# Banks for the output projection's transposes, scores of the last groups, a third begun step and halved sums in an attention + MLP kernel

## Chip, cores and metric

One core of one Trainium2 chip runs the whole program. The metric is device time in microseconds (us) of one execution. The engines are TensorE (PE, with its weight loads as PEld), VectorE (DVE), ScalarE (ACT), GpSimd (POOL) and SyncE (SP), which issues the DMAs. PE writes its results to PSUM, which has eight banks of 128 rows x 512 fp32 values; DVE and ACT read them there.

## What is computed

A pre-norm transformer layer in fp32: 2048 tokens, width 512, 32 heads of 16, and an MLP of width 1792 with SiLU.

```python
def _A_ref(x, wqkv, wo):                       # attention
    qkv = (x @ wqkv).reshape(B, S, 3, H, Dh).transpose(2, 0, 3, 1, 4)
    q, k, v = qkv[0], qkv[1], qkv[2]
    p = softmax(einsum("bhqd,bhkd->bhqk", q, k) * Dh ** -0.5)
    o = einsum("bhqk,bhkd->bhqd", p, v)
    return o.transpose(0, 2, 1, 3).reshape(B, S, D) @ wo
def _B_ref(x, w1, w2):                         # MLP
    return silu(x @ w1) @ w2
h  = x + _A_ref(layernorm(x), wqkv, wo)
h2 = h + _B_ref(layernorm(h), w1, w2)
```

## The kernel before

**Stages.** The first 200 us normalize and turn the tokens and project q, k and v. Then attention runs in 32 *items*. An item is four heads with one block of 512 queries (items 0 to 7 are block 0, 8 to 15 block 1, and so on) and has 16 *groups*, one for each chunk of 128 keys, numbered c = 0 to 15. A group is four score matmuls (`scores`, L536, tile `ps_s`), each followed by an exponential on ACT that writes `pt`, and, two groups later, four matmuls with the values into the bank `pv` (`values`, L547).

**Maxima.** The softmax needs each row's maximum before its scores are made. Score tiles are therefore also made the other way round, with queries on the rows (`maximum`, L210, tile `ps_m`), and DVE reduces each to one column of `mx`. An item takes 64 of them. They are made one to two items ahead, at most three in a group, between the scores (L957 to L965). When an item's 64 are done, `finish_max` combines them, mostly on POOL, and `place_max` (L248) some steps later turns them on PE (`ps_n`), copies them (`mt`) and stores them by two DMAs into the query tile `qs`. How many steps later is said by `due_at` (L283); a step is a group, or inside an MLP one of its 14 slices (`tick`).

**The other work of a block.** When the items of block b are through, the next block's first item (items 8, 16 and 24) carries the output projection of block b in its groups c = 10 to 15: `output(b, n)` (L752) with n = c - 10. For n < 4 it projects one tile of 128 tokens (12 matmuls, `ps_wo`, with three maxima after the sixth where n < `MORE[b]`, which is 2, 2, 0) and adds the residual on DVE (`add_rows`, tile `ot`), then takes the statistics; for n = 1 to 4 it normalizes tile n - 1 (`hx`); for n = 2 to 5 it turns tile n - 2 by four PE transposes (`ps_tr`), which ACT copies rounded to `hth`, and from which DVE subtracts that for the remainder `htl` (`turn`, L173). So a tile `ps_tr` is free again once DVE has made `htl`. In a group the order on every engine is: the four scores with the maxima between them, then `output`, then the values of two groups before. After that item the MLP of the block runs (`mlp`, L701), 14 slices of two matmul groups of 12, with maxima of later items between them.

**The last block** has no attention to hide behind. `finish_last` (L780) finishes the last item, projects four token tiles, normalizes and turns them, and runs the MLP. The first layer's slices 0 and 1 are *begun by halves* (`begun`, `begin(f, m)`): 12 matmuls on the first 256 tokens as soon as those are turned, and 12 on the others. The last slice of the second layer adds the result to the rows on DVE and stores 128 rows at a time (`second`, L685).

**Order.** All instructions of an engine, and the DMAs on SP's queue, stay in the order in which the program calls them (`keep_in_program_order`). An instruction that waits holds back all that stands behind it on its engine.

**PSUM banks.** From the attention on there are three kinds, and a tile is taken by `bank(name, kind)`:

```python
open_banks(ctx, 2, pv=1, sm=3, st=4)            # L522
def bank(name, kind="st", dtype=F32): ...       # L132
```

`pv` is the accumulator of the values, and the MLP's first layer uses it too. The three banks `sm` are the *banks of maxima*: `ps_m`, `ps_n`, and some scores around the MLP. The four banks `st` are the *banks of scores*: `ps_s`, `ps_wo`, `ps_tr`, and the MLP's accumulators. A tile that asks for a bank while all of its kind are in use gets one whose reader is still to come, and its first matmul waits for that reader.

**SBUF.** The exponentials `pt` share 12 buffers (`bp`), which the MLP's activations use as well; split weights (a rounded part and a remainder) have two buffers for each kind (`gp`).

Of the kernel before, what the change touches and what calls it, by code (L numbers as in the profile page):

```python
# [11 lines left out]
F32R = mybir.dt.float32r  # L12
# [3 lines left out]
ALU = mybir.AluOpType  # L16
# [4 lines left out]
P = 128  # L21
S = 2048
D = 512
# [7 lines left out]
KC = S // P  # L31
# [20 lines left out]
WAIT = 2  # L52
# [13 lines left out]
MORE = 2, 2, 0  # L66
# [5 lines left out]
def attention_mlp_kernel(ctx: ExitStack, tc: tile.TileContext, x, wqkv, wo, w1, w2, out):  # L72
    nc = tc.nc
    x = x.flatten_outer_dims()
    out = out.flatten_outer_dims()
# [19 lines left out]
    def dve(fn, *a, **k):  # L95
        pin(getattr(nc.vector, fn)(*a, **k))  # L96

    def dma(*a):
        pin(nc.sync.dma_start(*a))  # L99
# [32 lines left out]
    def bank(name, kind="st", dtype=F32):  # L132
        return banks[kind].tile([P, 512], dtype, tag=kind, name=name)
# [36 lines left out]
    def normalize(dst, rows, mv, rs):  # L170
        dve("tensor_scalar", dst, rows, mv[:, 0:1], rs, op0=ALU.subtract, op1=ALU.mult)

    def turn(src, dst_h, dst_l):  # L173

        ps = bank("ps_tr").rearrange("p (c n) -> p c n", n=P)
        for c in range(4):
            tr(ps[:, c, :], src[:, c * P:(c + 1) * P], ident)
        act("copy", dst_h, ps)
        low(dst_l, ps, dst_h)
# [85 lines left out]
    END = 64 * ITEMS  # L265
    at = {"item": 0, "done": 0, "half": 0, "step": 0, "due": 0, "attention": False, "group": None, "ready": 0, "next": 0, "blocks": True}
# [16 lines left out]
    def due_at(i):  # L283

        g = at["group"]
        if g is None:
            return WAIT
        joint = g + WAIT + (JOINT - g - WAIT) % KC
        return joint - g if joint < KC * i - 2 and joint // KC - 1 not in (-1, *FIRSTS) else WAIT

# [26 lines left out]
    def weave(steps, inserts):  # L317

        for k, _ in enumerate(steps):
            if k + 1 in inserts:  # L320
                inserts[k + 1]()


    with ExitStack() as pa:
# [128 lines left out]
        for t in range(4):  # L453
# [4 lines left out]
            if t > 0:  # L458
                ps = turn_high(1, t - 1)
# [49 lines left out]
        for g in range(1, NG // 2):  # L509
            for m, (b, key) in enumerate([(b, 1) for b in range(NB)] + [(b, 0) for b in range(NB)]):  # L510
# [4 lines left out]
                n = 8 * g + m - 12  # L515
# [117 lines left out]
            else:  # L633
                dma(w, w2[f * P:(f + 1) * P, :])

    def split_weights(kind, f, engine, high="act"):
        if f < FC:
            w = raw_w.pop((kind, f))
            wh, wl = ws[kind, f] = [gp.tile([P, 512], F32R, name=kind + part) for part in "hl"]
            if high == "act":  # L640
                act("copy", wh, w)
            else:
                dve("tensor_copy", wh, w)
            low(wl, w, wh, engine)
# [27 lines left out]
        return statistics(h)  # L672

    def turn_rows(t):
        turn(hx.pop(t), hth[:, :, t * P:(t + 1) * P], htl[:, :, t * P:(t + 1) * P])

    def gate(ps, engine="dve"):
        g, gh, gl = (bp.tile([P, 512], dt, tag="pt", name=name)
# [6 lines left out]
    def second(b, acc, f, gh, gl, inserts={}):  # L685
        w2h, w2l = ws.pop(("w2", f))
        while f == 0 and len(acc) < 4:
            acc.append(bank("ps_acc"))
        steps = (product(acc[t], lambda c: gh[:, t * P:(t + 1) * P], lambda c: gl[:, t * P:(t + 1) * P],
                         lambda c: w2h, lambda c: w2l, 1, start=f == 0, stop=f == FC - 1) for t in range(4))  # L690
        if f < FC - 1:
            weave(chain.from_iterable(steps), inserts)
            return
        for t, step in enumerate(steps):
            weave(step, {k - 3 * t: fn for k, fn in inserts.items()})
            n = 4 * b + t
            h = rows_of(b, t)
            dve("tensor_tensor", h, acc[t], h, ALU.add)
            dma(out[n * P:(n + 1) * P, :], h)

    def mlp(b):  # L701

# [49 lines left out]
    def output(b, n):  # L752

        if n < 4:
            ps = bank("ps_wo")
            weave(project_rows(n, ps), {6: lambda: burst(3)} if n < MORE[b] else {})
            found[n] = add_rows(b, n, ps)
        if 0 < n < 5:
            normalize(hx[n - 1], rows_of(b, n - 1), *found.pop(n - 1))
        if 1 < n < 6:  # L760
            turn_rows(n - 2)
# [18 lines left out]
    def finish_last(pending):  # L780
        b = NB - 1
        for g in pending:
            values(g)
        pvs = last.pop()

        o_t = bp.tile([P, 4, P], F32, tag="pt", name="o_t")
        pool("memset", o_t[:, :, :64], 0.0)
        act("activation", small.tile([P, 1], F32, name="sw"), ident[:, :1], AF.Silu)
        ps_rows = [bank("ps_wo", "sm") for _ in range(3)] + [bank("ps_wo")]
        first = [project_rows(t, ps_rows[t], range(3), stop=False) for t in range(4)]  # L790

        def some(t, n):
            for _ in range(n):
                next(first[t])

        def rest(t):
            run(first[t], project_rows(t, ps_rows[t], [DC - 1], start=False))

        some(0, 3)
        ps_q, ps_o = (bank(name).rearrange("p (t n) -> p t n", n=P) for name in ("ps_q", "ps_o"))  # L800
        for t in range(4):
            tr(ps_q[:, t, :], pvs[:, t * P:(t + 1) * P], ident)
        rc = small.tile([P, 4, 4], F32, name="rl", bufs=1)
        heads = ps_q.rearrange("p t (k r) -> p t k r", r=32)
        dve("reciprocal", rc, heads[:, :, :, DH])
        for j in range(2):

            to = o_t[:, :, 64:].rearrange("p t (k d) -> p t k d", d=DH)[:, :, 1 - j::2, :]
            dve("tensor_tensor", to, heads[:, :, j::2, :DH],
                rc[:, :, j::2, None].to_broadcast([P, 4, 2, DH]), ALU.mult)  # L810
        some(0, 6)
        for t in range(4):
            tr(ps_o[:, t, :], o_t[:, t, :], ident)
        ps_o = ps_o.rearrange("p t n -> p (t n)")[64:]
        act("copy", hth[64:, DC - 1, :], ps_o)
        low(htl[64:, DC - 1, :], ps_o, hth[64:, DC - 1, :])
        found, parts = {}, {}
        begun = [bank("ps_w1") for _ in range(2)]

        def add(t):  # L820
            h = rows_of(b, t)
            dve("tensor_tensor", h, ps_rows[t], hx[t], ALU.add)
            found[t] = statistics(h)

        def norm(t):
            normalize(hx[t], rows_of(b, t), *found[t])

        def turn_first(t):
            ps = bank("ps_tr", "sm").rearrange("p (c n) -> p c n", n=P)
            for c in range(4):  # L830
                tr(ps[:, c, :], hx[t][:, c * P:(c + 1) * P], ident)
            h = hth[:, :, t * P:(t + 1) * P]
            act("copy", h, ps)
            parts[t] = ps, h

        def turn_second(t):
            ps, h = parts[t]
            low(htl[:, :, t * P:(t + 1) * P], ps, h)

        def begin(f, m):  # L840

            cols = slice(m * 2 * P, (m + 1) * 2 * P)
            w1h, w1l = (w.rearrange("p (c n) -> p c n", n=P) for w in ws["w1", f])
            steps = [(w, hth, c) for c in range(DC) for w in (w1h, w1l)] + [(w1h, htl, c) for c in range(DC)]
            for n, (w, x, c) in enumerate(steps):
                mm(begun[f][:, cols], w[:, c, :], x[:, c, cols], start=n == 0, stop=n == len(steps) - 1)

        some(1, 5)
        rest(0)
        rest(1)  # L850
        add(0)
        add(1)
        norm(0)
        some(2, 9)
        turn_first(0)
        norm(1)
        rest(2)
        turn_first(1)
        add(2)
        turn_second(0)  # L860
        turn_second(1)
        rest(3)
        norm(2)
        begin(0, 0)
        turn_first(2)
        add(3)
        begin(1, 0)
        turn_second(2)
        norm(3)
        turn_first(3)  # L870
        turn_second(3)
        begin(0, 1)
        begin(1, 1)
        acc, waiting = [], []
        for f in range(FC):
            load_weights("w1", f + 3)
            load_weights("w2", f)
            if f < 2:
                ps = begun[f]
            else:  # L880
                ps = bank("ps_w", "sm")
                w1h, w1l = (w.rearrange("p (c n) -> p c n", n=P) for w in ws["w1", f])
                run(product(ps, lambda c: w1h[:, c, :], lambda c: w1l[:, c, :],
                            lambda c: hth[:, c, :], lambda c: htl[:, c, :], DC))
            waiting.append((f, *gate(ps)))
            split_weights("w1", f + 2, "dve")
            if f:
                split_weights("w2", f - 1, "dve")
            if f > 1:
                second(b, acc, *waiting.pop(0))  # L890
        split_weights("w2", FC - 1, "dve")
        while waiting:
            second(b, acc, *waiting.pop(0))
# [27 lines left out]
    for g in range(groups):  # L921
# [38 lines left out]
        for m in range(4):  # L960
            k = m ^ (g % 2)
            if (g, k) not in pts:
                scores(g, k)
            if skip <= m < skip + n:
                one_max(1 - HEADS[k][1])  # L965
        if i in FIRSTS and c > OUTPUT:
# [37 lines left out]
```

## Time and profile before

| | |
|---|---|
| runs | 1691.54, 1692.24, 1692.86 us (median 1692.24) |
| the profiled execution | 1694.05 us, of which the profile spans 1692.3 |
| mean granted PE clock | 0.998 |
| PE busy | 1660.4 us (98%) |
| DVE busy | 1455.0 us (86%), of it 1257.4 in 2009 reductions of maxima |
| ACT busy | 1242.2 us (73%), of it 1012.8 in 2048 exponentials |
| POOL busy | 269.7 us (16%) |

Lines of the profile name an instruction by the kernel's line and engine, its operation, and `out<-in` by the program's tile names with buffer numbers left out; "x3" is a count, and a time in brackets is how long the engine stood idle before it and what ended that. Since the matmuls, copies and DMAs are called through helpers, most PE lines read L79 (L82 for transposes), ACT lines L93, DVE lines L96 (L219 for the maxima) and DMA lines L99: the tile tells which it is. The MLP's begun slices and its first slice are all shown as `ps_w`. Matmuls overlap, so that the time from one start to the next, and not the duration shown, is what one costs PE.

### The profile page before, as it was taken

The numbers are of one execution on the slowest core, as the hardware profiler recorded it, in microseconds if no ns is written. First come the engines' busy times: TensorE is split into PE (matmuls) and PEld (weight loads), VectorE is DVE, ScalarE is ACT, GpSimd is POOL, SyncE is SP. The second block draws the span as 40 slices with busy tenths as digits, with TensorE's granted clock in tenths as the row PEclk, the third lists the DMA queues.
The fourth block names the chain that finished last, engine by engine and source line by source line (L and its number), as shares of the span: only waits on it lengthen the run. The fifth ranks groups of instructions, "written<-read, shape, count | busy, mean of one in ns | idle before, by whom it ended". The sixth has DMA issues, their size and how long they took to land.

```text
span 1692.3 us, 28327 instructions
## 1 busy us (share of the span) xinstructions
PE 1660.4 (98%) x10498; PEld 645.5 (38%) x10498; DVE 1455.0 (86%) x2428; ACT 1242.2 (73%) x2443; POOL 269.7 (16%) x441
## 2 busy tenths in 40 slices
PE   7999999999999999999999999999999999999999
PEld 6666422222245532222245532222245542222377
DVE  6899999999978889999978889999978889997343
ACT  5323599999963279999953369999963379999743
POOL 3123400000033310000033310000034310000000
PEclk9999999999999999999999999999999999999999
DMA  4434311121222111111222211111222211100222
GB/s 175 118 82 156 113 34 41 37 50 38 63 59 89 59 49 32 36 50 38 61 59 80 69 49 32 36 44 44 60 61 79 69 49 31 35 11 20 58 82 81
DMA packets 100618, 102.81 MB, mean 61 GB/s; under 512 B 19076, under 2 KB 77252, under 8 KB 100480
## 3 DMA queue, kind: packets, MB, share of 16 engines
q1 hardware_dynamic: 100480, 101.01, 20.4%
q8 instruction: 82, 1.34, 0.3%
q14 instruction: 56, 0.46, 0.1%
HBM read 77.72 MB, written 17.29 MB: 56 GB/s over the span
## 4 chain that ended last, share of the span: by engine, by line
PE 88%; ACT 7%; DVE 3%; DMA 1%; issue 1%; SPq 0%; POOL 0%; ACTq 0%; POOLq 0%
PE pv L79 34%; PE ps_s L79 19%; PE ps_m L79 11%; PE ps_acc L79 10%; ACT pt L93 6%; PE ps_qk L79 5%; PE ps_wo L79 3%; PE ps_v L79 3%; PE ps_w L79 2%; DVE mx L219 2%; PE ps_tr L82 1%; SPq L99 0%; DVE pvs L96 0%; DMA ks<-in_A_x_dram 0%; DMA ks<-kd 0%
## 5 line engine op out<-in xcount | busy, mean ns | idle before, releaser
L219 DVE TENSOR_REDUCE mx<-ps_m 128x1 f32<-128x512 f32 x2009 | 1257.4, 682 | 89.1 <-PE ps_m L79 63.1
L93 ACT ACTIVATE pt<-ps_s 128x512 f32<-128x512 f32 x2048 | 1012.8, 608 | 21.8 <-PE ps_m L79 14.9
L79 PE MATMUL ps_s<-qs,ks 64*128 64x512 f16 x2048 | 535.6, 379 | 5.5 <-ACT pt L93 2.4
L79 PE MATMUL pv<-pt,va 128*17 128x512 f32 x4096 | 538.2, 599 | 1.2
L79 PE MATMUL ps_m<-ks,qs 48*128 48x512 f16 x2009 | 506.7, 381 | 4.1 <-DVE mx L219 3.6
L79 PEld LDWEIGHTS <-ks 64*128 64x128 f16 x2048 | 148.8, 94 | 546.9 <-issue 437.6
L79 PEld LDWEIGHTS pv<-pt,va 128*17 128x17 f32 x4096 | 68.7, 95 | 227.4 <-issue 209.8
L79 PEld LDWEIGHTS <-qs 48*128 48x128 f16 x2048 | 118.4, 94 | 69.0 <-issue 64.2
L93 ACT CAST w2h<-w 128x512 fp32r<-128x512 f32 x56 | 34.8, 621 | 101.8 <-PE ps_acc L79 101.8
L93 ACT ACTIVATE g<-pv 128x512 f32<-128x512 f32 x39 | 23.3, 597 | 102.2 <-PE pv L79 102.2
L79 PE MATMUL ps_acc<-w2l,gh 128*128 128x512 f32 x224 | 92.8, 414 | 0.0
L79 PE MATMUL ps_acc<-w2h,gh 128*128 128x512 f32 x224 | 91.8, 410 | 0.0
L79 PE MATMUL ps_acc<-w2h,gl 128*128 128x512 f32 x224 | 88.0, 393 | 0.0
L86 POOL TENSOR_TENSOR w2l<-w,w2h 128x512 fp32r<-128x512 f32 x42 | 53.7, 1280 | 164.4 <-ACT w2h L93 164.4
L96 DVE TENSOR_TENSOR gl<-g,gh 128x512 fp32r<-128x512 f32 x53 | 37.0, 699 | 48.5 <-ACT gh L93 48.5
L93 ACT ACTIVATE ks<-ps_qk,qk_s 128x512 f32<-128x512 f32 x30 | 20.7, 689 | 71.7 <-PE ps_qk L79 68.8
L79 PE MATMUL pv<-htl,w1h 128*128 128x512 f32 x156 | 65.5, 420 | 0.0
L86 POOL TENSOR_SCALAR nm<-nm 128x16 f32<-128x16 f32 x51 | 12.9, 253 | 328.5 <-DVE nm L229 325.2
L86 POOL TENSOR_TENSOR mx<-mx 128x32 f32<-128x32 f32 x38 | 9.5, 250 | 345.2 <-DVE mx L219 343.6
L79 PE MATMUL pv<-hth,w1h 128*128 128x512 f32 x156 | 62.3, 399 | 0.0
L86 POOL TENSOR_TENSOR ot<-ot,den 128x512 f32<-128x512 f32 (+1 forms) x16 | 20.4, 1274 | 257.9 <-DMA den<-dr 227.1
L79 PE MATMUL pv<-hth,w1l 128*128 128x512 f32 x156 | 61.3, 393 | 0.0
(125 smaller groups left out, 1386.3 us busy)
## 6 DMA issues: line engine op xcount, KB each, us to landing
w<-in_B_w_dram SPq DMA_DIRECT2D x112, 256.0 KB
ks<-kd SPq DMA_DIRECT2D x120, 192.0 KB
qs<-qd SPq DMA_DIRECT2D x128, 48.0 KB
kd<-sh SPq DMA_DIRECT2D x16, 256.0 KB
qd<-sh SPq DMA_DIRECT2D x16, 256.0 KB
hx<-in_A_x_dram SPq DMA_DIRECT2D x16, 256.0 KB
out_dram<-ot SPq DMA_DIRECT2D x16, 256.0 KB
ot<-pvs SPq DMA_DIRECT2D x124, 32.0 KB
```

The lines of the kernel that those rows point to most:

```text
L79: tc.keep_in_program_order(nc.tensor.matmul(*a, **k))
L82: tc.keep_in_program_order(nc.tensor.transpose(*a))
L86: tc.keep_in_program_order(getattr(nc.gpsimd, op)(*a, **k))
L93: pin(getattr(nc.scalar, fn)(*a, **k))
L96: pin(getattr(nc.vector, fn)(*a, **k))
L219: pin(nc.vector.tensor_reduce(mx[i][:, j, a, qt, kb:kb + 1], ps, axis=AX.X, op=ALU.max))
```

## The change

1. **Banks in the output projection.** `turn` gets a parameter for the kind of bank, and `turn_rows` passes "sm": the transposes of the output projection take a bank of maxima. The projection itself takes one too for n >= `MORE[b]`, that is for two of four tiles in the first two blocks and for all four in the third.
2. **Place of the maxima.** `due_at` returns 3 instead of 2 steps inside the MLP.
3. **Last groups.** Once all maxima are made (`at["done"] == END`), scores 2 and 3 of a group take banks of maxima.
4. **Last MLP.** A third slice is begun by halves; its weights are split before the projections' second tile, into two of the `pt` buffers, instead of after the first slice's activation.
5. **Last sum.** The last 128 rows are added and stored in two halves of 256 columns. (`rows_of` is called before the matmuls instead of after them, which emits nothing.)

```diff
-    def turn(src, dst_h, dst_l):
-
-        ps = bank("ps_tr").rearrange("p (c n) -> p c n", n=P)
+    def turn(src, dst_h, dst_l, kind="st"):
+
+        ps = bank("ps_tr", kind).rearrange("p (c n) -> p c n", n=P)
...
         if g is None:
-            return WAIT
+            return WAIT + at["attention"]
...
-    def split_weights(kind, f, engine, high="act"):
+    def split_weights(kind, f, engine, high="act", pt=False):
...
-            wh, wl = ws[kind, f] = [gp.tile([P, 512], F32R, name=kind + part) for part in "hl"]
+            wh, wl = ws[kind, f] = [bp.tile([P, 512], F32R, tag="pt", name=kind + part) if pt else
+                                    gp.tile([P, 512], F32R, name=kind + part) for part in "hl"]
...
-        turn(hx.pop(t), hth[:, :, t * P:(t + 1) * P], htl[:, :, t * P:(t + 1) * P])
+        turn(hx.pop(t), hth[:, :, t * P:(t + 1) * P], htl[:, :, t * P:(t + 1) * P], "sm")
...
-            dve("tensor_tensor", h, acc[t], h, ALU.add)
-            dma(out[n * P:(n + 1) * P, :], h)
+            parts = 1 + (n == KC - 1)
+            for m in range(parts):
+                cols = slice(m * D // parts, (m + 1) * D // parts)
+                dve("tensor_tensor", h[:, cols], acc[t][:, cols], h[:, cols], ALU.add)
+                dma(out[n * P:(n + 1) * P, cols], h[:, cols])
...
-            ps = bank("ps_wo")
+            ps = bank("ps_wo", "st" if n < MORE[b] else "sm")
...
-        begun = [bank("ps_w1") for _ in range(2)]
+        begun = [bank("ps_w1") for _ in range(3)]
...
+        split_weights("w1", 2, "dve", pt=True)
         some(1, 5)
...
         norm(3)
+        begin(2, 0)
         turn_first(3)
         turn_second(3)
-        begin(0, 1)
-        begin(1, 1)
+        for f in range(3):
+            begin(f, 1)
...
-            if f < 2:
+            if f < 3:
                 ps = begun[f]
...
-            split_weights("w1", f + 2, "dve")
+            if f:
+                split_weights("w1", f + 2, "dve")
...
-                scores(g, k)
+                scores(g, k, "sm" if at["done"] == END and m > 1 else "st")
```

More of the change, by code (lines that the diff above doesn't have):

```diff
@@ L694, in second @@
         for t, step in enumerate(steps):
-            weave(step, {k - 3 * t: fn for k, fn in inserts.items()})
             n = 4 * b + t
             h = rows_of(b, t)
-            dve("tensor_tensor", h, acc[t], h, ALU.add)
-            dma(out[n * P:(n + 1) * P, :], h)
+            weave(step, {k - 3 * t: fn for k, fn in inserts.items()})
+            parts = 1 + (n == KC - 1)
[3 more added lines that the diff above has]
+                dma(out[n * P:(n + 1) * P, cols], h[:, cols])
     def mlp(b):
```

## Prediction

> **What bounds the kernel now.** I read the page first, then the stretches by stage, then the waits of TensorE (PE), and last the timelines where the edits lie.
>
> ```profile
> span 1692.3 us, 28327 instructions
> PE 88%; ACT 7%; DVE 3%; DMA 1%; issue 1%; SPq 0%; POOL 0%; ACTq 0%; POOLq 0%
> ...
> 469.00:501.30 32.30, 30.36 (x181) 13.90 (x177) 25.88 (x47) 19.50 (x37) 10.23 (x16) 1.00 0.23 66
> 501.30:614.00 112.70, 111.96 (x497) 65.04 (x496) 96.01 (x158) 40.27 (x69) 39.95 (x46) 1.00 0.21 63
> ```
>
> The columns of the stretches are the length, then busy time of PE, weight loads, DVE, ACT and POOL, clock and DMA. PE holds 88% of the chain. In the first block's output projection (469 to 501) it stands still for 1.9 us, more than the MLP behind it (0.7 in 113 us), so a PE wait there is paid in full. What PE's scores and projections wait for in the whole span (us, times, longest):
>
> ```profile
> PE ps_s L79 <- ACT pt L93: 2.4, 8, 0.5
> PE ps_wo L79 <- ACT pt L93: 1.9, 3, 0.6
> ...
> PE ps_s L79 <- DVE htl L96: 0.9, 3, 0.3
> ```
>
> These are the waits for banks of scores that the first edit is about.
>
> **Output projection and transposes in banks of maxima.** There are four banks for scores and three for maxima. The first block at c = 12 and 13 (a row of several instructions gives its first start and the whole time, xcount):
>
> ```profile
> 482.94 0.50 PE L79 MATMUL ps_wo<-wo_h,oh 128*128 128x512 f32 x1
> 483.03 1.88 DVE L219 TENSOR_REDUCE mx<-ps_m 128x1 f32<-128x512 f32 x3
> ...
> 486.10 0.69 DVE L96 TENSOR_TENSOR ot<-ps_wo,hx 128x512 f32<-128x512 f32 x1 [1.19 <-POOL ol L86]
> ...
> 487.58 0.59 PE L79 MATMUL ps_s<-qs,ks 64*128 64x512 f16 x2
> ...
> 487.78 2.07 ACT L93 ACTIVATE pt<-ps_s 128x512 f32<-128x512 f32 x4 [0.20 <-PE ps_m L79]
> 487.81 0.38 PE L79 MATMUL ps_m<-ks,qs 48*128 48x512 f16 x1
> ...
> 488.08 0.68 DVE L96 TENSOR_TENSOR htl<-ps_tr,hth 128x512 fp32r<-128x512 f32 x1
> 488.43 0.37 PE L79 MATMUL ps_s<-qs,ks 64*128 64x512 f16 x1 [0.25 <-ACT pt L93]
> 488.68 1.87 DVE L219 TENSOR_REDUCE mx<-ps_m 128x1 f32<-128x512 f32 x3
> 488.92 0.50 PE L79 MATMUL ps_wo<-wo_h,oh 128*128 128x512 f32 x1
> ```
>
> What the edit aims at is the fourth score at 488.43. Two scores take 0.59 and one 0.37, so PE's steps here are 0.22; behind the third maximum at 487.81 it could have stood at 488.03. The transposes hold a bank of scores until `htl` ends at 488.76, and the score takes the bank of the first exponential of its own group instead, which ends 0.62 after 487.78. That is 0.40 lost. It also tells how banks are given: to the one released first, not in turn.
>
> Now each step with the new banks. At c = 12 the group's three maxima fill all three banks when the projection of tile 2 asks for one. DVE ends the first maximum at 483.03 + 0.68 = 483.71 (three in 1.88, 0.60 apart), so the projection starts at 483.76, not 482.94: **+0.82**. At c = 13 one maxima bank holds the transposes of tile 0. The first two maxima of the group find room (the projection's bank is read out by 486.10 + 0.69); the third gets the transposes' bank, as DVE reads it before any maximum of this group. It waits for 488.76 and starts at 488.81, a full 1.00 after 487.81. The fourth score, behind it in PE's order, starts 0.22 later at 489.03, where 488.43 stood. Tile 3's projection needs the first maximum read: 488.68 + 0.68, so 489.41 for 488.92: **+0.49**. The last two groups:
>
> ```profile
> 494.06 0.68 DVE L96 TENSOR_TENSOR htl<-ps_tr,hth 128x512 fp32r<-128x512 f32 x1
> ...
> 494.66 1.87 DVE L219 TENSOR_REDUCE mx<-ps_m 128x1 f32<-128x512 f32 x3
> 494.89 0.66 PE L82 MATMUL ps_tr<-ident,hx 128*128 128x128 f32 x4
> ...
> 496.91 0.68 DVE L96 TENSOR_TENSOR htl<-ps_tr,hth 128x512 fp32r<-128x512 f32 x1
> 496.92 0.38 PE L79 MATMUL ps_m<-ks,qs 48*128 48x512 f16 x1
> ...
> 497.60 0.37 PE L79 MATMUL ps_s<-qs,ks 64*128 64x512 f16 x1 [0.31 <-DVE htl L96]
> 498.10 0.66 PE L82 MATMUL ps_tr<-ident,hx 128*128 128x128 f32 x4
> ```
>
> c = 14 is the same: the third maximum waits for 494.74, and the next transposes, now in a maxima bank, for the first maximum's end at 495.34: 495.39 for 494.89, **+0.50**. At c = 15 DVE comes 0.5 earlier against PE, since its `htl` hangs on the last projection alone and not on the wait just counted; the third maximum loses some 0.2 where the fourth score lost 0.46, and the last transposes come sooner by **0.36**. One block: 0.82 + 0.49 + 0.50 - 0.36 = 1.45. The second block shows the same pattern. In the third all four projections move:
>
> ```profile
> 1231.42 4.60 DVE L219 TENSOR_REDUCE mx<-ps_m 128x1 f32<-128x512 f32 x7
> ...
> 1234.76 0.37 PE L79 MATMUL ps_s<-qs,ks 64*128 64x512 f16 x1
> 1235.76 0.50 PE L79 MATMUL ps_wo<-wo_h,oh 128*128 128x512 f32 x1 [0.63 <-ACT pt L93]
> ...
> 1240.47 1.85 DVE L219 TENSOR_REDUCE mx<-ps_m 128x1 f32<-128x512 f32 x3
> 1240.82 0.50 PE L79 MATMUL ps_wo<-wo_h,oh 128*128 128x512 f32 x1
> ```
>
> The seven maxima end at 1236.02, the first of the last three at 1234.82, so tile 0's projection follows the score at once, 0.36 behind it: 1235.12 for 1235.76, **-0.64**. Tile 1 waits for 1240.47 + 0.66: **+0.36**. With 0.82, 0.49, 0.50 and -0.36 as above: +1.17. Together 1.45 + 1.45 + 1.17 = **+4.1**. Behind each wait stand all of PE's work and, through it, DVE's and ACT's, which idle then (DVE 1.19 before 486.10). Bounds: if no maxima bank is ever late, the fourth scores' 0.40, 0.40 and 0.46 of each block and the 0.64 are all saved, -4.4; if a group's first maximum got the transposes' bank instead of its third, +9.8 (rival below). I take the value between, as it follows DVE's order.
>
> **Place of the maxima one step later in the MLP.**
>
> ```profile
> 1276.88 1.87 DVE L219 TENSOR_REDUCE mx<-ps_m 128x1 f32<-128x512 f32 x3
> ...
> 1277.61 0.22 PE L82 MATMUL ps_n<-ident_h,ns 128*32 128x128 f16 x1 [0.66 <-DVE mx L219]
> ```
>
> The small transpose finds three maxima in its banks and waits until DVE has read the first, at 1277.56. One step later DVE has caught up. The product behind it, 0.15 after it, can then start when its own bank is read, by DVE's instruction before these three, at about 1277.0; the burst inside it then finds its third bank 0.2 late. A DVE copy of 32 rows and two short stores into `qs` move with it by a step of about 8 us (113 us for 14); the scores that need them are made after the MLP. I take -0.55, and -0.15 for the ends of the other two MLPs, where the transpose leaves a crowded group: **-0.7**, between -0.9 and +0.2 (the same wait meets it a step later).
>
> **Scores of the last groups.**
>
> ```profile
> L93 ACT ACTIVATE pt<-ps_s 128x512 f32<-128x512 f32 x61 | 30.1, 696 | 0.0
> ...
> 1589.46 2.16 ACT L93 ACTIVATE pt<-ps_s 128x512 f32<-128x512 f32 x4
> ...
> 1590.90 0.71 ACT L93 ACTIVATE pt<-ps_s 128x512 f32<-128x512 f32 x1
> ```
>
> Within a group exponentials start (1590.90 - 1589.46) / 3 = 0.480 apart; over 61 of them (30.1 - 0.70) / 60 = 0.490. The difference is the step to the next group, whose first score waits behind work that waited for a bank of scores. With two scores of four in the idle maxima banks that goes: 80 exponentials by 0.010 to 0.012, -0.9. Against it, the score right behind the very last maximum (about 1548.6) now asks for a bank that DVE still holds, 0.5 of delay that ACT has no store for. **-0.3**; from -0.9 to +0.5.
>
> The Trainium skill (ScalarE: Activation LUTs, What ACT_TABLE_LOAD costs) gives an activation 186 ns + 0.833 ns per element, with 93 ns of overlap back to back: worked out as an estimate, 520 ns for 512 elements. By it ACT itself would set the pace and this edit would be worth nothing; the trace's 480 is shorter, and decides.
>
> **The last MLP's third step.**
>
> ```profile
> 1609.26 0.63 PE L79 MATMUL ps_w<-htl,w1h 128*128 128x256 f32 x4
> 1610.44 0.63 PE L82 MATMUL ps_tr<-ident,hx 128*128 128x128 f32 x4 [0.55 <-DVE hx L96]
> 1611.74 0.39 PE L79 MATMUL ps_w<-hth,w1h 128*128 128x256 f32 x1 [0.67 <-ACT hth L93]
> ...
> 1617.61 0.68 DVE L96 TENSOR_TENSOR w2l<-w,w2h 128x512 fp32r<-128x512 f32 x1
> 1618.75 0.39 PE L79 MATMUL ps_acc<-w2h,gh 128*128 128x512 f32 x1
> ```
>
> A half step is 12 matmuls 0.115 apart, 1.4. The first half fills the gap from 1609.72 to 1610.44 and puts the last transposes off by 0.7, and with them 1611.74; three halves behind that end at 1616.7. The accumulation could then start 2 us earlier than 1618.75, but the low half of its weights comes out of DVE behind the second step's gate, and this starts some 0.4 later: the 0.7, less 0.3 in which ACT now copies a weight that will have been copied early. So `w2l` ends at 1618.29 + 0.4 = 1618.7; the third matmul, which needs it, stood two steps behind 1618.75, at 1619.2: **-0.5**. Bounds: -2 (weights in time), +0.7 (only the delay). The early split's copy and subtraction fall into idle ACT and DVE around 1597; uncovered they would cost 0.7. Its loads are old ones, and the queue gets a slot free sooner.
>
> **The last sum in halves.**
>
> ```profile
> 1686.25 2.73 DVE L96 TENSOR_TENSOR ot<-ps_acc,ot 128x512 f32<-128x512 f32 x4 [2.28 <-PE ps_acc L79]
> ```
>
> Two sums of half the width end some 0.1 later than one of 0.69 (four take 2.73, 0.68 apart); the last store carries half the bytes but is one more to issue and to wait for. No row prices it; I put it at **-0.1**, within 0.3 either way, less than half a sum.
>
> **The sum**: 4.1 - 0.7 - 0.3 - 0.5 - 0.1 = +2.5. The profiled execution took 1694.05 with 1.8 around its span of 1692.3, and would take 1696.5; the runs' median, 1692.24, lies 1.8 below it, so 1694.7.
>
> **Rivals.** *Maxima banks are free in time* (faster): if DVE reads the maxima sooner than PE asks, -4.4 in place of +4.1 gives 1686.2. For it: the scores' waits exist, eleven of them. Against: the DVE rows end after PE's natural starts by 0.8 to 1.0, and PE is served in order. *The transposes' bank goes to a group's first maximum* (clearly slower): the first is two steps of 0.22 ahead of the third, so at c = 13 and c = 14 PE stands 0.5 longer with all the group behind it, and at c = 15 the 0.36 is lost and 0.5 more: 1.9 a block, 1700.4 in all three; with one block alone it already passes the bound of slower. Against: releases go in DVE's order. *ACT sets the last groups' pace*: only the 0.5 delay of that edit stays out of its gain, +0.8 against the sum, 1695.5.
>
> **How the numbers follow.** The forecast has a chance of 0.48 (its own range 1692.2 to 1697.0), the first rival 0.15, the second 0.24, the third 0.13. What a measurement can tell from no change is 0.2%, 3.4 us: 1688.9 to 1695.6. Of the forecast three quarters lie inside and a quarter above; of the third rival half and half; the second is above; the first below. Faster 0.15, same 0.43, slower 0.42. The range 1687.5 to 1698.5 leaves out most of the first rival and the far half of the second, 0.2.
>
> **What would show it.** PE waits of `ps_m` for `htl` near 1.0 at c = 13 and 14 and of `ps_wo` for `mx` near 0.8 at c = 12 in all blocks, and none of `ps_s` for `pt` there; the small transpose without a wait in the third MLP; exponentials 0.48 apart after 1551; the first `ps_acc` of the last MLP about 0.5 earlier against the end of attention. If the three output projections are not longer by 1 us or more each, the prediction is wrong at its main step.

## The result and the profile after

Twelve runs of each kernel: before 1692.25 us (1691.54 to 1694.23), the changed kernel 1696.58 us (1694.73 to 1698.18). The ratio is 1.0024, 95% interval 1.0016 to 1.0031, so the change costs 4.1 us (2.7 to 5.2). 1694.7 was predicted, with 1687.5 to 1698.5 as the range: the time lies inside, on the side of slower, and above the forecast.

The page of the changed kernel, its span and the chain that ended last:

```profile
span 1695.8 us, 28366 instructions
PE 87%; DVE 4%; ACT 4%; issue 2%; POOL 1%; DMA 1%; SPq 0%; DVEq 0%; ACTq 0%; POOLq 0%
```

PE and ACT lost shares of the chain (88% and 7% before), DVE and issue gained (3% and 1% before). The same count of matmuls takes longer where the transposes and projections are. The stretches of the changed kernel, cut at the same instructions as the two of before in the prediction, then the third output projection with its surroundings, first before, then after (length; busy time of PE, weight loads, DVE, ACT, POOL; clock; DMA):

```profile
468.25:502.02 33.77, 30.86 (x181) 13.91 (x177) 25.98 (x47) 19.82 (x37) 10.22 (x16) 1.00 0.22 64
502.02:614.75 112.73, 111.99 (x497) 65.13 (x496) 96.09 (x158) 40.27 (x71) 39.95 (x46) 1.00 0.22 63
```

```profile
1226.00:1264.00 38.00, 36.06 (x227) 15.29 (x224) 29.02 (x51) 26.30 (x51) 11.38 (x14) 1.00 0.24 65
```

```profile
1228.36:1267.52 39.16, 36.50 (x227) 15.29 (x224) 29.04 (x51) 26.57 (x50) 11.37 (x14) 1.00 0.23 64
```

The first projection takes 33.77 for 32.30 (+1.47), the MLP behind it 112.73 for 112.70. The third projection takes 39.16 for 38.00 (+1.16), the second one +1.48 by the same cut. And the waits of PE in the whole span, those that the change made, moved or shrank:

```profile
PE ps_m L79 <- DVE htl L96: 3.8, 6, 0.6
...
PE ps_wo L79 <- DVE mx L219: 3.0, 4, 0.9
PE ps_s L79 <- ACT pt L93: 2.0, 3, 1.0
...
PE ps_acc L79 <- ACT w2h L93: 1.0, 1, 1.0
...
PE ps_s L79 <- DVE mx L219: 0.7, 2, 0.4
PE ps_acc L79 <- DVE w2l L96: 0.2, 1, 0.2
```

Before, each of the three projections had two waits of scores for `pt` and one for `htl`, 0.8 together, for which the banks were exchanged. None of them is left there. Of the 2.0 still in the list, 1.03 lies ahead of the second projection, at 851.80, behind a copy on ACT that POOL kept waiting; in the runs below, with this edit and without it, that wait is 0 to 0.47. The rest lies elsewhere too. In their place stand ten longer waits behind DVE, 3.8 of `ps_m` for `htl` and 3.0 of `ps_wo` for `mx`. The first block's, one by one (PE's and DVE's rows in order of time):

```profile
483.01 0.50 PE L79 MATMUL ps_wo<-wo_h,oh 128*128 128x512 f32 x1 [0.86 <-DVE mx L219]
...
488.15 0.68 DVE L96 TENSOR_TENSOR htl<-ps_tr,hth 128x512 fp32r<-128x512 f32 x1
...
488.89 0.37 PE L79 MATMUL ps_m<-ks,qs 48*128 48x512 f16 x1 [0.64 <-DVE htl L96]
...
489.11 0.38 PE L79 MATMUL ps_s<-qs,ks 64*128 64x512 f16 x1
...
489.49 0.50 PE L79 MATMUL ps_wo<-wo_h,oh 128*128 128x512 f32 x1
```

The profiled execution of this kernel runs 0.75 ahead here, so before's clock is this one's plus 0.75. The projection of tile 2 starts at 483.76 on it, the third maximum at 489.64, the fourth score at 489.86, tile 3's projection at 490.24. Against the starts of before (482.94, 487.81, 488.43, 488.92) these are +0.82, +1.83, +1.43 and +1.32. Each step's own part is the difference from the one ahead: +0.82; then +1.01 - 0.40 - 0.11 = +0.50 from tile 2 to tile 3. The next group gives +0.50 again and the last -0.35.

Not all of a span's difference belongs to the change. The first exponential of the attention starts 1.3 us sooner in this profiled execution, though no edit touches what is ahead of it, and in the runs below it lies between 1.7 sooner and 1.0 later than before's. The granted clock differs as well: over 190 to 230 us its mean is 0.91 here and 0.96 before, and over 840 to 885 us it is 0.96 in both, but 1.00 in nine of the twelve runs below. So each term below is read as a shift between neighbouring instructions, not from spans.

### The profile page after: what moved, and what is told of

Its sections match the earlier page's. It is cut to its first block, busy times and chain, and to the rows that moved or that the text cites. A ratio compares the mean times of both kernels' runs of the same rounds, so it can differ in the third digit from the quotient of the medians.

```text
span 1695.8 us, 28366 instructions
## 1 busy us (share of the span) xinstructions
PE 1660.8 (98%) x10510; PEld 644.2 (38%) x10510; DVE 1456.3 (86%) x2429; ACT 1243.2 (73%) x2443; POOL 269.6 (16%) x441
## 4 chain that ended last, share of the span: by engine, by line
PE 87%; DVE 4%; ACT 4%; issue 2%; POOL 1%; DMA 1%; SPq 0%; DVEq 0%; ACTq 0%; POOLq 0%
PE pv L79 34%; PE ps_s L79 20%; PE ps_m L79 11%; PE ps_acc L79 10%; PE ps_qk L79 5%; ACT pt L93 4%; PE ps_v L79 3%; PE ps_w L79 2%; DVE mx L219 2%; PE ps_wo L79 1%; PE ps_tr L82 1%; DVE ot L96 1%; DVE st L96 1%; DVE pvs L96 0%; POOL ol L86 0%
```

## Experiments

Runs with a ratio were executed eleven times, beside 15 to 21 executions of the kernel before, which spread from 1690.8 to 1694.4 us. The others were executed once, with a trace: `wo_only` 1695.03, `tr_only` 1696.11, `before_norm` 1693.20, `sc_only` 1692.54, `sc_next` 1693.60, `due_only` 1693.33, `third_only` 1693.79 and `third_w2` 1691.15 us. Against that spread these single times can't carry a term of 1 us. Only `wo_only` and `tr_only` lie above it, and which of the two costs more can't be read from their times either: ahead of the first projection, where their edits have no part, the one trace is 1.20 ahead of before's and the other 1.35 behind. So the terms of these runs are read from their traces.

**1 and 2. The banks alone, and everything but the banks.** The first edit put into the kernel before (`a_only`), and taken out of the changed kernel (`without_a`):

```diff
-        turn(hx.pop(t), hth[...], htl[...])
+        turn(hx.pop(t), hth[...], htl[...], "sm")
...
-            ps = bank("ps_wo")
+            ps = bank("ps_wo", "st" if n < MORE[b] else "sm")
```

> The kernel before with the first edit alone: transposes and projections of the output projection in banks of maxima. Theory (PE waits there for DVE's maxima and low halves): each of the blocks longer by what the changed kernel shows, +0.82, +0.50, +0.50, -0.35 in the first two and -0.70, +0.37, +0.82, +0.50, +0.50, -0.35 in the third, 4.1 us in all, ratio 1.0024. Rival (the sum of the other edits carries the loss, and the banks only shift waits from place to place): within 1 us of before, ratio 1.0006 or less.

> The changed kernel with that first edit undone and the other four kept. Theory: 4.1 us less than the changed kernel, so about the time of before: last scores +0.45, third step -0.3, place of maxima -0.1, last sum 0.0, in all 0.0, ratio 1.0000. Rival: the loss stays, ratio 1.002 or more.

Alone: 1696.58 us against 1692.71, ratio 1.0022 (1.0013 to 1.0031). In the trace the three projections are longer by 1.48, 1.49 and 1.15, 4.12 in all (the first one from its first matmul to its last transposes: 471.90 to 500.11 for 471.37 to 498.10). Without it: 1692.11, ratio 0.9995 (0.9986 to 1.0004). The whole loss is the banks of the output projection; the other four edits together can't be told from nothing.

**3 and 4. Which use of the banks.** `wo_only` has the second line of the diff above, `tr_only` the first.

> The kernel before with the projections alone in banks of maxima, the transposes in banks of scores as before. Theory: in the first two blocks the projection of tile 2 waits 0.82 for the first maximum, that of tile 3 0.49, and nothing behind: 1.3 each; in the third block -0.70 + 0.37 + 0.82 + 0.49 = 1.0; 3.6 us in all. No wait of ps_m for htl. Rival (each of the two uses has its own price and they add up to 4.1): then the transposes alone cost 0.5.

> The kernel before with the transposes alone in banks of maxima. Theory: no wait at tile 2; the third maximum of the two groups with a transposed tile behind them waits for the low half (ps_m for htl, six times, 0.6 each) and puts what follows off by 0.5 each, the last transposes come 0.35 sooner: 0.65 in each block, 1.9 us in all. With the projections alone at 3.6 the two parts would add up to 5.5, more than the 4.1 of both, since at tile 3 one wait serves for both. Rival (they add up): 0.5 us.

PE's waits in the first block (460 to 510 us), the projections alone first, then the transposes alone:

```profile
PE ps_wo L79 <- DVE mx L219: 1.5, 2, 0.9
PE ps_s L79 <- ACT pt L93: 0.9, 3, 0.3
PE ps_wo L79 <- ACT pt L93: 0.6, 1, 0.6
PE ps_m L79 <- DVE mx L219: 0.2, 1, 0.2
```

```profile
PE ps_m L79 <- DVE htl L96: 1.3, 2, 0.6
PE ps_wo L79 <- ACT pt L93: 0.6, 1, 0.6
PE ps_m L79 <- DVE mx L219: 0.2, 1, 0.2
```

Up to the last transposes the projections alone cost 1.41, 1.38 and 1.08 in the three blocks (3.87; 3.6 expected), the transposes alone 0.56, 0.57 and 0.56 (1.69; 1.9 expected). Together that is 5.56, not 4.12: at tile 3 the projection's wait for the first maximum and the third maximum's wait for `htl` are two ways of waiting for one stretch of DVE's work, and whoever waits first has waited for both. Adding up is out.

**5 and 6. DVE's order.** If PE waits for DVE's place in its own order, less work ahead of the maxima must shorten the waits. The normalisation of tiles 0 and 1 (0.52 each) was put behind the next group's maxima, once in the changed kernel (`late_norm`) and, as a control, in the kernel before (`before_norm`):

```diff
 def output(b, n):
+    if 1 < n < 4:
+        normalize(hx[n - 2], rows_of(b, n - 2), *found.pop(n - 2))
...
-        if 0 < n < 5:
+        if 2 < n < 5:
             normalize(hx[n - 1], rows_of(b, n - 1), *found.pop(n - 1))
```

> The changed kernel, with the normalisation of the first two token tiles of each output projection put on DVE behind the next group's maxima instead of ahead of them (one instruction of 0.52 each; all arithmetic stays). Theory (PE waits for DVE's maxima there, so their place in DVE's order is the price): the maxima come 0.43 sooner at tile 2 and at tile 3, PE's wait of 0.86 for the first one falls to 0.43 and the third maximum's for the low half from 0.64 to about 0.2; -0.86 in each block, -2.6 us in all against the changed kernel, ratio to before 1.0008 to 1.0010. Rival (a bank short, whatever DVE's order): no change from the changed kernel, 1.0024.

> The kernel before, with the normalisation of the first two token tiles put behind the next group's maxima, as in the run with the changed kernel: a control. Theory (the 0.9 a block that this saved there were waits of the banks of maxima): with the banks of scores PE doesn't wait for those maxima, so each output projection changes by less than 0.2. Rival (the maxima limit PE there in any case): -0.9 in each block, -2.6 us.

The same two waits of the first block, in the changed kernel with the late normalisation:

```profile
482.12 1.85 DVE L219 TENSOR_REDUCE mx<-ps_m 128x1 f32<-128x512 f32 x3
...
482.83 0.50 PE L79 MATMUL ps_wo<-wo_h,oh 128*128 128x512 f32 x1 [0.40 <-DVE mx L219]
...
487.54 0.66 DVE L96 TENSOR_TENSOR htl<-ps_tr,hth 128x512 fp32r<-128x512 f32 x1
...
488.25 0.37 PE L79 MATMUL ps_m<-ks,qs 48*128 48x512 f16 x1 [0.18 <-DVE htl L96]
```

0.86 has become 0.40, and 0.64 has become 0.18. The three projections now cost 0.57, 0.56 and 0.24 over before, 2.7 less than the changed kernel's 4.11; the time is 1693.14, ratio to before 1.0006 (0.9997 to 1.0015). In the kernel before, the same reorder takes 0.19, 0.20 and 0.19 off, at the edge of the "less than 0.2" that was expected. So some 0.7 of the 0.9 per block is DVE's order seen through the banks of maxima. Banks short whatever DVE's order, the rival, would have left the waits as they were. What is left of the cost, 1.4 us in all, still stands beside waits for DVE (in the whole span of `late_norm`, 1.6 of `ps_wo` for `mx` and 2.5 of `ps_m` for `htl`).

**7 and 8. Scores of the last groups.** The edit alone, and begun one group later, when no bank waits for a maximum:

```diff
+        spare = at["done"] == END      # sc_next: asked ahead of the group
         for m in range(4):
...
-                scores(g, k)
+                scores(g, k, "sm" if at["done"] == END and m > 1 else "st")   # sc_only
+                scores(g, k, "sm" if spare and m > 1 else "st")               # sc_next
```

> The kernel before with two scores of four of the last groups in banks of maxima, alone. Forecast's theory (banks set the pace of the exponentials): -0.3 us between the last maximum and the end of attention. Rival (ACT's own pace): the 0.5 us of delay behind the last maximum stays to the end, +0.45 us there.

> The same edit, but from the group behind the last maximum on, so that no score waits for a bank that DVE still reads. Forecast's theory: without that delay 80 exponentials gain 0.010 to 0.012 each, -0.8 us at the end of attention. Rival: ACT ends an exponential every 0.490 us with either set of banks; their starts may run ahead at 0.477 until the banks are full again, but the last one ends where it ended before: 0.0 us, and 0.45 less than the edit as it was made.

With the edit as made, the end of attention (the last values) comes 0.46 later against the last maximum; begun a group later, 0.07 sooner. The exponentials of this stage in one row each, first start and time from there to the last one's end; before, the changed kernel, and the edit begun later:

```profile
1549.84 41.78 ACT L93 ACTIVATE pt<-ps_s 128x512 f32<-128x512 f32 x85
```

```profile
1554.30 41.27 ACT L93 ACTIVATE pt<-ps_s 128x512 f32<-128x512 f32 x84 [0.43 <-PE ps_s L79]
```

```profile
1549.00 42.25 ACT L93 ACTIVATE pt<-ps_s 128x512 f32<-128x512 f32 x86
```

The first one of each row takes about 0.60. From its end to the last end are (41.78 - 0.60) / 84 = 0.490, (41.27 - 0.60) / 83 = 0.490 and (42.25 - 0.60) / 85 = 0.490. The pace of the ends is the same with seven banks as with four: it is ACT's own. PE doesn't set it: in the run begun later its groups of scores start at 1549.57, 1551.41, 1553.06 and 1554.87, so 1.65 to 1.84 apart, and only from there on 1.96, four times 0.490. What the added banks change is how far the starts run ahead, as the durations of single ones (ns, least, median, most) show, before and after:

```profile
L93 ACT ACTIVATE pt<-ps_s x85: 592/689/712, 1549.8 to 1590.9; 128x512 f32<-128x512 f32 x85
```

```profile
L93 ACT ACTIVATE pt<-ps_s x92: 592/1078/1137, 1549.9 to 1594.4; 128x512 f32<-128x512 f32 x92
```

For some 40 exponentials the starts stand 0.477 apart and the recorded duration of each grows by 0.013, the 0.490 - 0.477 that the ends lag; then the banks are full, and the starts fall back to 0.490 too. The wait in the second of the three rows, 0.43, is the price: the score behind the last maximum found its bank with DVE (`ps_s` for `mx`, 0.4), ACT stood still once, and nothing later makes up for it.

**9. The place of the maxima alone.**

```diff
-            return WAIT
+            return WAIT + at["attention"]
```

> The kernel before with the place of the maxima one step later in the MLP, alone. Theory from the changed kernel's trace: the wait of 0.66 in the third MLP goes, but 0.2 to 0.3 of it comes back at the step behind, and in the first two MLPs 0.44 saved at one step is paid again at the next: 0.0, 0.0 and -0.1 us in the three, and -0.4 in the groups right behind the second. Rival (forecast): -0.55 in the third MLP, -0.15 over the other two, none given back.

The first two MLPs are unchanged within 0.01, and the third is 0.10 shorter; in runs without this edit (`a_only`, `before_norm`, `sc_next`) it is up to 0.07 shorter too. The first groups behind the second MLP gain 0.43. There the small transpose held a bank of maxima until DVE, behind two sums, had copied it to `mt`, and a maximum waited 0.40 behind its score; one step later it stands 0.10 behind (before, then `due_only`):

```profile
995.97 0.37 PE L79 MATMUL ps_s<-qs,ks 64*128 64x512 f16 x1 [0.47 <-ACT pt L93]
...
996.11 0.20 DVE L96 COPY mt<-ps_n 32x128 f16<-32x128 f16 x1
...
996.37 0.37 PE L79 MATMUL ps_m<-ks,qs 48*128 48x512 f16 x1
```

```profile
995.74 0.37 PE L79 MATMUL ps_s<-qs,ks 64*128 64x512 f16 x1 [0.46 <-ACT pt L93]
...
995.84 0.37 PE L79 MATMUL ps_m<-ks,qs 48*128 48x512 f16 x1
```

In the third MLP of the changed kernel the place of the wait is seen (at the step of the old transpose and at the new one; this clock is before's plus 3.52):

```profile
1280.53 0.49 PE L79 MATMUL pv<-hth,w1h 128*128 128x512 f32 x1
...
1288.05 1.88 DVE L219 TENSOR_REDUCE mx<-ps_m 128x1 f32<-128x512 f32 x3
...
1288.36 0.39 PE L79 MATMUL ps_acc<-w2l,gh 128*128 128x512 f32 x1
...
1288.79 0.22 PE L82 MATMUL ps_n<-ident_h,ns 128*32 128x128 f16 x1
...
1288.93 0.50 PE L79 MATMUL pv<-hth,w1h 128*128 128x512 f32 x1
...
1289.27 0.39 PE L79 MATMUL pv<-hth,w1l 128*128 128x512 f32 x1
```

The old wait is gone, and the product starts 0.75 sooner than before's (1277.76 there, 1277.01 by before's clock), as soon as its own bank is read. But one step later DVE is behind again. It ends the first maximum at 1288.05 + 0.68 = 1288.73, and the transpose starts 0.43 after the matmul ahead of it, where PE's step is 0.23. That is a wait of 0.20 which the list of waits doesn't show. The transpose also costs PE its own time here: 0.14 up to the product, and 0.34 instead of 0.23 for the product's first matmul. PE's instructions behind it stand only 0.11 sooner than before.

**10 and 11. The third begun step, and its second weights.** The edit alone (`third_only`), and with the split of the second layer's first weights one slice earlier (`third_w2`):

```diff
-            if f:
-                split_weights("w2", f - 1, "dve")
+            if f != 1:
+                split_weights("w2", max(0, f - 1), "dve")
```

> The kernel before with the last MLP's third step begun by token tiles, alone. Theory (only the sums' start is moved, and it then waits for its own weights): first sum 0.87 earlier against the end of attention, 0.53 of that given back in waits of 1.0 for the high half of the second weights and 0.2 for the low half; 0.3 us in all from the end of attention to the end. Rival (the third begun step changes the end only through its transposes, 0.7 later): +0.4.

> The same edit, and the split of the second product's first weights (ACT copy, DVE low half) put one step earlier, behind the first gate: the work is the same. Theory (ACT's order keeps the sums waiting, not the transfer of the weights): the waits for those weights go, the first sum starts 1.0 to 1.5 earlier than with the third step alone, and the end comes 1.0 to 1.5 sooner; 1.3 to 1.8 less than before from the end of attention. Rival (DVE or the loads are the limit): no more than 0.3 gained over the third step alone.

The edit alone brings the first sum 0.86 sooner and the end 0.28. The changed kernel shows who takes the rest:

```profile
1620.56 0.61 ACT L93 CAST w1h<-w 128x512 fp32r<-128x512 f32 x1
1621.08 0.61 ACT L93 CAST w2h<-w 128x512 fp32r<-128x512 f32 x1
...
1621.74 0.49 PE L79 MATMUL ps_acc<-w2h,gh 128*128 128x512 f32 x1 [0.97 <-ACT w2h L93]
...
1622.63 0.50 PE L79 MATMUL ps_acc<-w2l,gh 128*128 128x512 f32 x1 [0.16 <-DVE w2l L96]
```

And with the split earlier:

```profile
1614.38 0.62 ACT L93 CAST w2h<-w 128x512 fp32r<-128x512 f32 x1
...
1615.86 0.39 PE L79 MATMUL ps_acc<-w2h,gh 128*128 128x512 f32 x1
1616.08 0.39 PE L79 MATMUL ps_acc<-w2h,gl 128*128 128x512 f32 x1
1616.31 0.40 PE L79 MATMUL ps_acc<-w2l,gh 128*128 128x512 f32 x1
```

`w2h` now ends 0.86 ahead of its matmul instead of holding it, no wait of the sums is left, and from the end of attention to the end it is 2.0 us less than before. So the place of the split in the engines' order was the limit, not the loads: ACT's copy by the wait of 0.97, and DVE's low half, which moves with it, by that of 0.16. The 2.0 is a little more than the 1.3 to 1.8 expected.

**12. What gained, put together.** The kernel before with the place of the maxima, the third begun step and the earlier split, without the banks, the last groups' scores and the halves.

> The kernel before with the parts that gained, and none that lost: place of maxima one step later (-0.55), third step begun with the weights' split one step earlier (-1.3 to -1.8). Theory: 1.8 to 2.3 us less than before, ratio 0.9986 to 0.9989. Rival (gains of this size are given back at the next wait): within 0.5 us of before, 0.9997 to 1.0003.

1689.61 us (1689.19 to 1690.82) against 1692.70, ratio 0.9983 (0.9974 to 0.9992): faster than both kernels. By the trace it is 2.0 from the last MLP, 0.06 from the third MLP and 0.42 from the groups behind the second, 2.5 in all. That is more than the 1.8 to 2.3 expected, and the runs' 2.9 (1.4 to 4.4) holds it.

## Why the prediction came out as it did

| term | predicted | changed kernel's trace | alone |
|---|---|---|---|
| output projections | 1.45 + 1.45 + 1.17 = +4.1 | 1.47 + 1.48 + 1.16 = +4.1 | +4.12 |
| place of the maxima | -0.7 | -0.5 | -0.53 |
| scores of the last groups | -0.3 | +0.47 | +0.46 |
| third begun step | -0.5 | -0.35 | -0.28 |
| last sum in halves | -0.1 | 0.0 | not run |
| sum | +2.5 | +3.7 | |

The terms of the trace sum to 3.7, and the runs' 4.1 (2.7 to 5.2) holds that. Of the 1.2 between the two sums, 0.8 is the scores of the last groups.

**The main step was right** in mechanism and size. Every shift of the first block came as worked out: 0.82, 0.49 (0.50 measured), 0.50, -0.36 (-0.35), and in the third block -0.64 (-0.70), +0.36 (+0.37). It rested on a bank going to whoever comes behind the reader released first, so that the third maximum, not the first, got the transposes' bank; the rival with the first (1.9 a block) and the rival of free banks are both out. The time alone wouldn't have told: the first of them in one block only gives 1694.7 + 1.9 = 1696.6, the measured time. A projection was longer by 1 us or more in each block, as asked for. Of the signs asked for, the waits "of `ps_m` for `htl` near 1.0" are starts that are 1.0 late, of which the view of waits lists 0.64.

**The scores of the last groups failed**, in the step "The difference is the step to the next group, whose first score waits behind work that waited for a bank of scores. With two scores of four in the idle maxima banks that goes". The 0.480 between starts within a group was taken for ACT's pace. The ends, 0.490 apart whatever the banks, are the pace, so only the 0.5 of delay was left, which the prediction had seen. That is the third rival: in this term it was right, and its 1695.5 is nearer to the measured 1696.6 than the forecast. The Trainium skill (ScalarE: Activation LUTs, What ACT_TABLE_LOAD costs), by which an estimate of 520 ns was set against 480, was put aside for the wrong reason. Its figure is 6% above the 490 of the ends, but that ACT itself sets the pace here was so.

**The place of the maxima** was sized nearly right by luck, from two errors that cancel. In the third MLP the 0.55 did come at the old step, and 0.44 of it went again one step later. "One step later DVE has caught up" failed there: 0.20 is the wait for DVE, the upper bound's case. The rest is the transpose's own cost to PE: the prediction took the 0.15 between transpose and product as saved and put nothing in its place at the new step. The end of the second MLP gave 0.41, where 0.15 was set for the other two together, as the copy out of the transpose's bank held a maximum there.

**The third step**: that DVE's low half, not PE, decides was right; the low half ends 0.40 later against the end of attention, as worked out, and the third matmul came 0.46 sooner where 0.5 was set. Behind its wait the step to the next matmul is 0.34 instead of 0.23, which leaves 0.35 for the end. The first matmul came 0.89 sooner, where the sign asked for 0.5. ACT's copy of the same weight, queued behind that for `w1h`, held the first matmul as well. The bound of -2 "weights in time" is what experiment 11 measured.

**The last sum** is within its bounds: from the last matmul group's last start to the end it is 4.42, for 4.40. It was not tried alone.

## What to carry to other kernels

A bank of PSUM is worth as much as its reader is early: moving PE's output to a kind of banks whose reader is a busy engine traded nine short waits (0.8 in each block) for ten longer ones here (6.8 in all), and the order of that reader's work then mattered more than the number of banks: two instructions of 0.52 in each block, moved, gave back 2.7 of the 4.1. Where instructions of an engine overlap, read its pace from the ends, not from the starts. A move of an instruction also has to be paid for at its new place. After a product is begun earlier, look at what it needs next: here the split of one weight, moved by one slice, was worth six times the edit itself (2.0 - 0.28 against 0.28).

## What the runs showed of the hardware

The starts of exponentials from PSUM run at 0.477 us as long as scores lie ready, while their ends keep 0.490; the recorded duration of one grew to 1.14 us that way, though ACT did no more work. ACT's copies from SBUF stand 0.52 apart (1620.56 and 1621.08 above). The Trainium skill (Perfetto Trace Analysis, Optimizing Scalar/DVE Operations) gives ACT a smaller fixed cost for PSUM than for SBUF, 51 against 93 ns; the two distances of starts, 0.477 and 0.52, differ by the same 0.04, so the trace agrees in that. A copy out of PSUM shows that it is the source and not the exponential: in the kernel before, the instruction behind it starts 0.48 later.

```profile
486.48 0.59 ACT L93 CAST hth<-ps_tr 128x512 fp32r<-128x512 f32 x1 [2.12 <-PE ps_tr L82]
486.96 0.62 ACT L93 CAST w1h<-w 128x512 fp32r<-128x512 f32 x1
```
